# Couples of half products in the prologue of an attention and MLP block, and maxima that end three steps ahead of a group's first score instead of four

## The chip, the cores and the metric

The kernel runs on one core of a Trainium2 chip. The metric is the time of one execution on the device in microseconds, as the median of several runs; less is better. Before the change it is 1688.64 us, the median of three runs (1687.62 to 1691.29).

## What is computed

One transformer block over 2048 tokens of width 512, in float32, with 32 heads of width 16 and a hidden width of 1792. The condition vector gives six rows that shift, scale and gate.

```python
    def _A_ref(x, wqkv, wo):
...
        scale = Dh ** -0.5
        scores = jnp.einsum("bhqd,bhkd->bhqk", q, k) * scale
        p = _softmax(scores, axis=-1)
        o = jnp.einsum("bhqk,bhkd->bhqd", p, v)
...
    sa, ca, ga, sb, cb, gb = (mod[:, 0], mod[:, 1], mod[:, 2], mod[:, 3], mod[:, 4], mod[:, 5])
    h = _layernorm(x, axis=-1) * (1 + ca) + sa
    x = x + ga * _A_ref(h, A_wqkv, A_wo)
    h = _layernorm(x, axis=-1) * (1 + cb) + sb
    x = x + gb * _B_ref(h, B_w1, B_b1, B_w2)
```

`_B_ref` is Dense, Mish (`h * tanh(softplus(h))`), Dense.

## The kernel before

**Numbers.** Products that need more precision than TensorE's fast float32 gives are made from a high and a low part of each factor: three products (high by high, high by low, low by high) in one PSUM bank. `hi_copy` and `lo_sub` (L87 to L96) make the parts.

**Groups and steps.** Queries come in 4 blocks of 512 rows, heads in 8 groups of 4, which makes 32 groups of work. The main loop, `step(t)`, has 16 steps for a group, T = 512 in all. A step makes four score products (L618, a 128-key block by 512 queries, for two pairs of heads), their exponentials on ACT (L621), and the products with the values of two steps earlier (L636). The softmax needs the greatest score of each query. It is found beforehand from separate products (L569, followed by a reduce on DVE, L571); `neg_max` (L587) joins the parts, `max_rows` (L596) transposes them, and its `put` (L603) sends the rows by four DMAs on SP's queue into two spare rows of the query operand `qa`, so that a score product subtracts them itself. Maxima run PRO = 16 + LEAD = 20 steps ahead of the scores, with LEAD = 4. So the main loop starts with a prologue of 20 steps, t = -20 to -1, of maxima alone (`max_pair`, L575: two 64-row products into two adjacent banks, and one reduce, L585, over both), and ends with 20 steps of scores without maxima.

**Halves.** Score and maximum products use 64 of TensorE's 128 rows. The products of two heads lie in the two halves of the array and run beside each other. Dense products, those of the projections and the MLP, use all 128 rows. In the prologue they are issued whole by `whole_units` (L1291), up to 7.2 products of 512 columns (CREDIT) in each step, after the step's maxima. From t = 0 on each dense product is cut into two halves by `mm_half` (L129); each runs beside a score or a maximum in the other half of the array, the first half in an even step, the second in the next odd one. Two halves of one product add into the same bank, so the first of the second halves is given a dependency on an instruction of ACT that came after the first halves.

**How a step is filled.** `next_part` (L1272) gives every couple of steps (even, odd) `f` dense slots, six where there is dense work and none where there is none. A step has four maxima and four scores. `maxima` (L1310) deals the maxima out: 4 - o to the one half of the array (`mo`) and o to the other (`alone`), where o is `max(0, (8 - f) // 2)`: one with six dense slots, four with none. With PRO even, the two steps that share a set of maxima are also the two that share f.

**What sets the order.** There is no scheduler: every engine's queue is in the order in which the code is written. `at(h, f)` defers a function to half step h (`run_hooks`). Units of dense work stand in one queue in the order of `plan` (L1426): value, query and key projections of the later column slices, then weights and MLP. `planned` (L1431) asks for the split of a weight slice (`slice_split`, L233) into high and low part, which ACT casts and POOL subtracts, and for the next slice's load. `clear`, `store_at` and `load_at` (L188 to L199) move stores and loads away from the half steps around `put`.

**Buffers.** PSUM has eight banks: a ring of six for scores and maxima (`ring`, L151), `ms` and `acc`. A dense unit's `fin` empties its bank: for a query or key unit ACT copies it to `qf` (L258) and POOL makes `qh` and `ql` (L259, L260), each with two buffers, which DMAs then store; a value unit is copied once (L287).

Of the kernel before, what the change touches and what calls it, by code (L numbers as in the profile page):

```python
# [8 lines left out]
F32 = mybir.dt.float32  # L9
# [9 lines left out]
def adaln_block(ctx: ExitStack, tc: tile.TileContext, x, wqkv, wo, w1, b1, w2, c, w_mod, out):  # L19
# [18 lines left out]
    LEAD = 4  # L38
# [4 lines left out]
    CREDIT = 7.2  # L43
    LATE_SPLIT = {3: -8, 4: 4}
    LATE_LOAD = {3: -15, 4: -4, 5: 9}
# [101 lines left out]
    ring_at = [0]  # L147

    kept = []

    def ring(w=1):  # L151
        if w == 2 and ring_at[0] % 2:
            ring_at[0] += 1
        if kept and ring_at[0] % NRING == NRING - 1:
            ring_at[0] += 1
        b = ring_at[0] % NRING
        ring_at[0] += w
        return ring_t[:, b, :] if w == 1 else ring_t[:, b:b + 2, :]

    def bank(tag="ms"):  # L160
        return ring() if tag == "ring" else ps.tile([P, TB], F32, tag=tag, name="bk", bufs=1)

    def free_banks():
# [3 lines left out]
        for i in nc.cur_bb.bb.instructions:  # L167
# [12 lines left out]
            if banks:  # L180
                for j, b, others, theirs in seen[-32:]:
                    if j.engine != i.engine and not banks & b and not names & theirs and not made & others:
                        tc.declare_no_dep(i, j, reason="other banks")
                seen.append((i, banks, names, made))
# [3 lines left out]
    def clear(h):  # L188

        return h if h < 60 or h % 32 < 25 else h - h % 32 + 34  # L190

    def store_at(h):

        h = clear(h)
        return h if h < 60 or h % 32 < 22 else h - h % 32 + 27

    def load_at(h):

        return h if h < 60 or 4 <= h % 32 < 20 else h - h % 32 + 28 if 20 <= h % 32 <= 28 else h + -(h - 4) % 32  # L199
# [23 lines left out]
    slices = {}  # L223
    put_away = set()
# [17 lines left out]
    def qk_unit(kind, ct, tb, tag):  # L242
# [7 lines left out]
        def fin(h=None):  # L250
            qh = qp.tile([P, TB], F32R, tag="qh", name="qh", bufs=2)
            ql = qp.tile([P, TB], F32R, tag="ql", name="ql", bufs=2)
            if h is None:
                hi_copy("a", qh, acc)
                lo_sub("v", ql, acc, qh)
            else:
                qf = pw.tile([P, TB], F32, tag="raw", name="qf", bufs=1)
                nc.scalar.copy(qf, acc)  # L258
                hi_copy("p", qh, qf)  # L259
                lo_sub("p", ql, qf, qh)  # L260
# [314 lines left out]
    def max_pair(n, jq, kb):  # L575
# [9 lines left out]
        nc.vector.tensor_reduce(out=mxs[n][:, :, jq, kb:kb + 1], in_=pm, op=ALU.max, axis=AX.X)  # L585

# [722 lines left out]

    def maxima(n, u, s, others):  # L1310

        j, qs = divmod(u, 4)
        return ([max_tile(n, j, s, qs, kb) for kb in range(4 - others)],
                [max_tile(n, j, 1 - s, qs, kb) for kb in range(4 - others, 4)])

    def step(t):
# [4 lines left out]
        if t < 0:  # L1321

            for i in range(2):
                if tm < 16:
                    kb, jq = divmod(2 * tm + i, 8)
                else:
                    jq, kb = tm % 16 // 2, 2 * second + i
                max_pair(tm // 16, jq, kb)
            if second and tm % 16 == 15:
                neg_max(tm // 16)  # L1330
            run_hooks(2 * t + 1)
            for f in ats.pop(t, []):
                f()
            whole_units(2 * t + 1, CREDIT)
# [7 lines left out]
        if not second:  # L1342
            first_of["part"] = []
            if t == T - PRO:
# [12 lines left out]
        if tm < T:  # L1357
            o = max(0, (8 - f) // 2)
            mo, alone = maxima(tm // 16, tm % 16 // 2, s, o)

            mine = [x for p in zip(mo, own) for x in p] + own[len(mo):]
        else:
            o = max(0, (4 - f) // 2)
# [62 lines left out]
    plan = [(-PRO, 2, 0, range(4, 16)), (-PRO, 0, 1, (0,)), (-PRO, 1, 1, range(NB)), (-PRO, 1, 2, range(NB)),  # L1426
# [4 lines left out]
    def planned(i, a, tag):  # L1431
# [3 lines left out]
        def fin(h):  # L1435
            if a == args[-1]:
                if i + 2 < len(plan):
                    d = 4 if h > 0 else 1
                    split_at[i + 2] = LATE_SPLIT.get(i + 2, h + d)
                    at(split_at[i + 2], lambda: slice_split(*plan[i + 2][1:3], hi_eng="p" if h > 0 else "a"))  # L1440
# [60 lines left out]
    for i in range(EARLY):  # L1501
        at(3 * i - 37, lambda i=i: early_prep(i, 3 * i - 37))
# [25 lines left out]
    at(-3, lambda: load_v(0))  # L1528
# [9 lines left out]
    for pp, h in ((2, -22), (3, -2)):  # L1538
# [4 lines left out]

    for t in range(-PRO, T + 2):
# [35 lines left out]
```

## Time and profile before

| What | us |
|---|---|
| median of three runs | 1688.64 |
| the profiled execution's own time | 1688.32 |
| its span, from first to last instruction | 1686.5 |
| first maxima of the prologue | 47.45 |
| first scores | 98.95 |
| first step without maxima | 1530.80 |

The span is shorter than the execution's time by what lies before the first instruction and after the last. In the rows of the profile, PE is TensorE's matmuls, PEld its weight loads, DVE VectorE, ACT ScalarE, POOL GpSimd and SP the engine that issues the DMAs. A row of the timeline gives start, length, engine, line, operation, tiles and count, and in brackets how long the engine had been idle and what ended that. A matmul's length is from its start to its last result; since they are pipelined, the distance of two starts is the better measure of what one costs. A row of busy time by stretch gives each engine's busy time with its number of instructions, then the granted clock of TensorE, the DMA engines' busy share and GB/s.

### The profile page before, as it was taken

To read this page: it belongs to the slowest core of one execution; us is meant where nothing else is said; L and a number is where in the kernel's file an instruction comes from. 1 tells how busy PE (TensorE), PEld (TensorE's weight loads), DVE (VectorE), ACT (ScalarE), POOL (GpSimd) and SP (SyncE) were. 2 spreads that over 40 slices of the span, in tenths; PEclk is the share of its full clock that TensorE was granted. 3 is DMA by queue.
4 is the path that set the end of the run, shared out by engine and by line. 5 is a ranking of instruction groups with operands and counts; after the bars stand their busy time and mean duration, and the time that the engine had idled before them with its cause. 6 is when DMAs were issued, how large, how long until landed. Compare 5 with 4: busy or idle time off the path is not lost.

```text
span 1686.5 us, 33920 instructions
## 1 busy us (share of the span) xinstructions
PE 1670.4 (99%) x12491; PEld 924.4 (55%) x12491; DVE 1432.9 (85%) x2372; ACT 1357.4 (80%) x2612; POOL 812.5 (48%) x839
## 2 busy tenths in 40 slices
PE   8999999999999999999999999999999999999998
PEld 6755655555445455555555455555555455555687
DVE  6998888888999988888889888888889888883377
ACT  7257777777778988888878998888878988889674
POOL 5555224655313664556323565556323664555442
PEclk9999999999999999999999999999999999999999
DMA  8877656777755334434355434534344433534261
GB/s 261 264 251 188 157 145 197 205 228 218 225 136 161 97 93 104 120 81 130 82 137 161 106 77 98 139 80 122 100 133 120 130 93 81 149 97 135 76 227 63
DMA packets 114983, 239.00 MB, mean 142 GB/s; under 512 B 24500, under 2 KB 50120, under 8 KB 108864
## 3 DMA queue, kind: packets, MB, share of 16 engines
q1 hardware_dynamic: 114808, 236.82, 49.7%
q8 instruction: 99, 1.62, 0.4%
q14 instruction: 68, 0.56, 0.1%
q10 hardware_dynamic: 8, 0.00, 0.0%
HBM read 180.48 MB, written 51.45 MB: 138 GB/s over the span
## 4 chain that ended last, share of the span: by engine, by line
PE 92%; DVE 3%; ACT 2%; DMA 1%; issue 1%; POOL 0%; SPq 0%; ACTq 0%; DVEq 0%; POOLq 0%
PE bk L636 29%; PE ring L618 22%; PE ring L569 19%; PE bk L134 11%; PE bk L127 3%; PE ring L127 2%; PE ring L1249 2%; DVE mx L571 2%; ACT pr L621 1%; PE ring L583 1%; DMA qa<-mt 0%; PE ring L952 0%; PE ring L598 0%; DMA xt<-in_A_x 0%; PE ring L134 0%
## 5 line engine op out<-in xcount | busy, mean ns | idle before, releaser
L571 DVE TENSOR_REDUCE mx<-ring 128x1 f32<-128x512 f32 x1968 | 1221.9, 681 | 150.9 <-PE ring L569 136.2
L621 ACT ACTIVATE pr<-ring 128x512 f32<-128x512 f32 x2048 | 1078.7, 603 | 207.8 <-PE bk L134 116.3
L569 PE MATMUL ring<-ka,qa 64*128 64x512 f32 x1968 | 818.3, 429 | 1.3 <-ACT pr L621 1.0
L618 PE MATMUL ring<-qa,ka 64*128 64x512 f32 x2048 | 759.0, 402 | 3.2 <-ACT pr L621 2.0
L636 PE MATMUL bk<-pr,vg 128*32 128x512 f32 x4096 | 545.1, 604 | 0.0
L569 PEld LDWEIGHTS ring<-ka,qa 64*128 64x128 f32 x1968 | 350.6, 184 | 326.4 <-DVE mx L571 251.4
L618 PEld LDWEIGHTS ring<-qa,ka 64*128 64x128 f32 x2048 | 373.6, 184 | 192.2 <-DVE mx L571 113.3
L134 PE MATMUL bk<-h,w 64*128 64x512 f32 (+1 forms) x1080 | 277.8, 390 | 0.0
L134 PE MATMUL bk<-w,a_h 64*128 64x512 f32 x632 | 210.8, 413 | 0.0
L134 PEld LDWEIGHTS bk<-h,w 64*128 64x128 f32 x1080 | 178.5, 184 | 9.2 <-ACT pr L621 1.5
L636 PEld LDWEIGHTS bk<-pr,vg 128*32 128x32 f32 x4096 | 81.2, 108 | 135.8 <-issue 126.5
L134 PE MATMUL bk<-w,a_l 64*128 64x512 f32 x316 | 124.0, 392 | 0.0
L134 PEld LDWEIGHTS bk<-w,a_h 64*128 64x128 f32 x632 | 106.7, 184 | 3.4 <-ACT hb L830 0.8
L1008 POOL TENSOR_TENSOR y<-yd,y 128x512 f32<-128x512 f32 x44 | 56.8, 1292 | 88.9 <-ACT yd L1007 79.5
L842 POOL TENSOR_SCALAR qq<-ee 128x512 f32<-128x512 f32 x25 | 15.5, 620 | 169.3 <-ACT ee L836 169.3
L858 POOL TENSOR_TENSOR qq<-qq,rr 128x512 f32<-128x512 f32 x42 | 54.1, 1289 | 85.8 <-ACT rr L852 85.8
L844 POOL TENSOR_TENSOR hb<-hb,ee 128x512 f32<-128x512 f32 x42 | 54.1, 1288 | 79.6 <-DVE ee L840 77.6
L134 PE MATMUL bk<-w,o_hl 64*128 64x512 f32 x288 | 79.3, 405 | 0.0
L96 POOL TENSOR_TENSOR a_l<-hb,a_h 128x512 fp32r<-128x512 f32 x53 | 73.1, 1379 | 4.4
L134 PEld LDWEIGHTS bk<-w,a_l 64*128 64x128 f32 x316 | 58.3, 184 | 2.8
L93 POOL TENSOR_SCALAR qh<-qf 128x512 fp32r<-128x512 f32 x27 | 16.7, 620 | 88.3 <-ACT qf L258 68.1
L134 PE MATMUL bk<-h_h,wl 64*128 64x512 f32 x168 | 57.3, 421 | 0.2 <-ACT pr L621 0.2
(222 smaller groups left out, 1901.3 us busy)
## 6 DMA issues: line engine op xcount, KB each, us to landing
ka<-kscr SPq DMA_DIRECT2D x124, 384.0 KB
w<-w2scr SPq DMA_DIRECT2D x56, 512.0 KB
w<-w1scr SPq DMA_DIRECT2D x46, 512.0 KB
vg<-vscr SPq DMA_DIRECT2D x32, 552.0 KB
qa<-qscr SPq DMA_DIRECT2D x124, 100.0 KB
kscr<-qh SPq DMA_DIRECT2D x16, 512.0 KB
qscr<-qh SPq DMA_DIRECT2D x32, 256.0 KB
w2scr<-hl SPq DMA_DIRECT2D x14, 512.0 KB
```

The costliest lines, as they stand in the source:

```text
L96: (nc.gpsimd if eng == "p" else nc.vector).tensor_sub(lo, src, hi.bitcast(F32))
L127: nc.tensor.matmul(acc, l, r, start=start, stop=stop)
L134: i = nc.tensor.matmul(acc, l[64 * g:64 * g + 64], r[64 * g:64 * g + 64], start=start and not then, stop=bool(stop and then))
L569: nc.tensor.matmul(pm, qt[64 * s:64 * s + 64, qs * P:(qs + 1) * P], kt[64 * s:64 * s + 64, kb * TB:(kb + 1) * TB], start=True, stop=True)
L571: nc.vector.tensor_reduce(out=mxs[n][:, s, 4 * j + qs, kb:kb + 1], in_=pm, op=ALU.max, axis=AX.X)
L618: nc.tensor.matmul(p_, kt[64 * s:64 * s + 64, kc * P:(kc + 1) * P], qt[64 * s:64 * s + 64, :], start=True, stop=True)
L621: e = nc.scalar.activation(pr, p_, AF.Exp, scale=SCALE)
L636: nc.tensor.matmul(accs[n][32 * h:32 * h + 32, :], vgs[n][:, o:o + 32], pts.pop((t, h)), start=(kc == 0), stop=(kc == 15))
L844: (nc.vector if tail else nc.gpsimd).tensor_mul(hb, hb, ee)
L858: nc.gpsimd.tensor_mul(qq, qq, rr)
L1008: nc.gpsimd.tensor_add(y[i], yd, y[i])
L1249: nc.tensor.matmul(po[i // 2][:, i % 2, :], l[:, s], w[:, r, :], start=(f == 0 and j == 0), stop=(f == FT - 1 and j == 2))
```

## The change

Three things go together.

**Couples.** In the prologue dense work is issued by `lanes`. It takes units until it has 12 slots (one query or key unit, or two value units in one bank), twice, and calls these two takes a couple. `turn(c, 0)` issues one half of each product of the first take beside the other half of each product of the second; `turn(c, 1)` the halves that are left, later. Two couples alternate over four banks: the last two of the ring (which is shortened to four in the prologue), `ms` and `acc`. Six couples make up the prologue, four slots after each pair of maxima. So that the second halves have something to wait for, the first pair of maxima after a first turn is followed by a small copy on ACT (`seen`).

**Lead.** LEAD is 3, PRO is 19. The prologue and the end lose a step each, the steps with both maxima and scores gain one. `put` comes two half steps later against the scores, and the limits in `clear`, `store_at` and `load_at` move by two. Because PRO is odd, the two steps that share a set of maxima now lie in different couples of steps; o is kept from the first of them, and where f differs the step has uneven halves.

**Order and tiles.** The query unit of the second column slice comes before the value units, the split of a slice is issued at once in the prologue, and units that finish just before t = 0 get tiles of their own (`late`) for their parts.

```diff
-    LEAD = 4
+    LEAD = 3
     PRO = 16 + LEAD
...
     def qk_unit(kind, ct, tb, tag):
...
         def fin(h=None):
-            qh = qp.tile([P, TB], F32R, tag="qh", name="qh", bufs=2)
-            ql = qp.tile([P, TB], F32R, tag="ql", name="ql", bufs=2)
+            late = h is not None and -4 <= h < 3
...
+            if late:
+                qh, ql = spares.pop(), spares.pop()
+            else:
+                qh = qp.tile([P, TB], F32R, tag="qh", name="qh", bufs=2)
+                ql = qp.tile([P, TB], F32R, tag="ql", name="ql", bufs=2)
...
         nc.vector.tensor_reduce(out=mxs[n][:, :, jq, kb:kb + 1], in_=pm, op=ALU.max, axis=AX.X)
+        if waiting:
+            seen = ap.tile([P, 2], F32, tag="seen", name="seen", bufs=2)
+            e = nc.scalar.copy(seen, pm[:, :, 0])
+            for c in waiting:
+                c["after"] = e
+            waiting.clear()
...
+    COUPLES = 6
+    now, waiting = [0], []
+    beds = [ring_t[:, NRING - 2, :], ring_t[:, NRING - 1, :], "ms", "acc"]
...
+        def turn(c, p):
+            (a, fa), (b, fb) = c["two"]
+            for j, both in enumerate(zip(a, b)):
+                for k in range(max(len(x) for x in both)):
+                    for x, g in zip(both, (p, 1 - p)):
+                        if k < len(x):
+                            mm_half(x[k], g, c["after"] if p and not j and not k else None, p)
+                yield len(a) - j - 1
+            if not p:
+                waiting.append(c)
+                return
+            for fin in fa + fb:
+                at(now[0] + 1, lambda fin=fin, h=now[0] + 1: fin(h))
+
+        for _ in range(COUPLES // 2):
+            c1 = yield from couple()
+            yield from turn(c1, 0)
+            c2 = yield from couple()
+            yield from turn(c2, 0)
+            yield from turn(c1, 1)
+            yield from turn(c2, 1)
...
+    def dense_slots(h, most):
+
+        now[0] = h
+        for _ in range(most):
+            if not next(lane, 0):
+                return
...
     def maxima(n, u, s, others):
 
         j, qs = divmod(u, 4)
+        if (n, u) == (1, PRO % 16 // 2):
+            return ([max_tile(n, j, v, qs, kb) for kb in (2, 3)] for v in (s, 1 - s))
...
+                dense_slots(2 * t + 1, 4)
             for f in ats.pop(t, []):
                 f()
-            whole_units(2 * t + 1, CREDIT)
...
-            o = max(0, (8 - f) // 2)
+            o = mst["others"] = max(0, (8 - f) // 2) if tm % 2 == 0 or not t else mst["others"]
             mo, alone = maxima(tm // 16, tm % 16 // 2, s, o)
 
             mine = [x for p in zip(mo, own) for x in p] + own[len(mo):]
+            m = len(mine)
+            if f > m:
+                mine = [mine[(i * m) // f] if (i + 1) * m // f > i * m // f else None for i in range(f)]
...
-    plan = [(-PRO, 2, 0, range(4, 16)), (-PRO, 0, 1, (0,)), (-PRO, 1, 1, range(NB)), (-PRO, 1, 2, range(NB)),
+    plan = [(-PRO, 0, 1, (0,)), (-PRO, 2, 0, range(4, 16)), (-PRO, 1, 1, range(NB)), (-PRO, 1, 2, range(NB)),
...
-                    at(split_at[i + 2], lambda: slice_split(*plan[i + 2][1:3], hi_eng="p" if h > 0 else "a"))
+                    split = lambda: slice_split(*plan[i + 2][1:3], hi_eng="p" if h > 0 else "a")
+                    split() if h < -4 else at(split_at[i + 2], split)
...
+    ring_of[0] = NRING - 2
```

Where the instructions stand, at three places. First TensorE's queue at the start of the prologue, before the change (`ka`, `qa` are keys and queries, so those rows are maxima; `bk` is `ms` or `acc`; 128x256 is a value unit's product):

```order
L583 MATMUL ring<-ka_98,qa_100 128x512 x4
L127 MATMUL bk<-wh,h_h 128x256 x4
L127 MATMUL bk<-wl,h_h 128x256 x4
L127 MATMUL bk<-wh,h_l 128x256 x4
L127 MATMUL bk<-wh,h_h 128x256 x2
L583 MATMUL ring<-ka_98,qa_100 128x512 x4
```

Four maxima (two pairs) and then whole products of value units. The same place after the change, where a row is a half product or several:

```order
L595 MATMUL ring<-ka_98,qa_100 128x512 x2
L133 MATMUL ring<-h_h,wh 128x512
L133 MATMUL ring<-wh,h_h 128x256 x2
L133 MATMUL ring<-h_h,wh 128x512
L133 MATMUL ring<-wh,h_h 128x256 x2
L133 MATMUL ring<-h_h,wh 128x512
L133 MATMUL ring<-wl,h_h 128x256 x2
L133 MATMUL ring<-h_h,wh 128x512
L133 MATMUL ring<-wl,h_h 128x256 x2
L595 MATMUL ring<-ka_98,qa_100 128x512 x2
```

One pair of maxima, then four slots, each a half of the query unit's product beside two halves of a value unit's; the query unit has come to the front.

Second, ACT's queue in the first part of the prologue, before (`wh<-wr` is the cast of a weight slice, `vq<-bk` and `qf<-bk` empty the banks of value units and of query and key units):

```order
L89 CAST qh<-ring 128x512
L89 CAST wh<-wr 128x512
L287 COPY vq<-bk 128x4x4x16 x12
L89 CAST wh<-wr 128x512
L258 COPY qf<-bk 128x512 x3
```

The cast of the key slice comes after all twelve copies of value units. After the change:

```order
L88 CAST qh<-ring 128x512
L88 CAST wh<-wr 128x512
L600 COPY seen<-ring 128x2 x2
L88 CAST wh<-wr 128x512
L270 COPY qf<-ring 128x512
L299 COPY vq<-ring 128x4x4x16 x2
L299 COPY vq<-bk 128x4x4x16 x4
L600 COPY seen<-ring 128x2 x2
```

The same cast now stands ahead of the copies that empty the first couple's banks.

Third, TensorE's queue in the main loop, in the step in which the first unit of the output projection starts after a stretch without dense work, before (t = 128; `w,o_hl` are halves of that unit, `qa,ka` scores, `ka,qa` maxima); it starts behind two pairs of a score and a maximum, which are left out:

```order
L134 MATMUL bk<-w_5827,o_hl 128x512
L618 MATMUL ring<-qa_101,ka_99 128x512
L134 MATMUL bk<-w_5827,o_hl 128x512
L569 MATMUL ring<-ka_701,qa_103 128x512
L134 MATMUL bk<-w_5827,o_hl 128x512
L618 MATMUL ring<-qa_102,ka_700 128x512
L134 MATMUL bk<-w_5858,o_hl 128x512
L569 MATMUL ring<-ka_701,qa_103 128x512
L134 MATMUL bk<-w_5858,o_hl 128x512 x2
L618 MATMUL ring<-qa_101,ka_99 128x512
L636 MATMUL bk<-pr,vg 32x512 x4
```

Maxima and scores take turns beside the dense halves. After the change the stretch ends two steps earlier, and the whole step (t = 126) reads:

```order
L133 MATMUL bk<-w_5980,o_hl 128x512
L636 MATMUL ring<-qa_104,ka_702 128x512
L133 MATMUL bk<-w_5980,o_hl 128x512
L636 MATMUL ring<-qa_100,ka_98 128x512
L133 MATMUL bk<-w_5980,o_hl 128x512
L133 MATMUL bk<-w_6009,o_hl 128x512
L636 MATMUL ring<-qa_104,ka_702 128x512
L133 MATMUL bk<-w_6009,o_hl 128x512 x2
L636 MATMUL ring<-qa_100,ka_98 128x512
L581 MATMUL ring<-ka_701,qa_103 128x512 x4
L654 MATMUL bk<-pr,vg 32x512 x4
```

Only scores run beside the dense halves, and all four maxima stand in a row at the step's end, in the half of the array that held the dense work.

70 lines of the change are left out of this document (52 added, 18 removed).

## The prediction

> **What bounds the kernel now.** The page comes first: its span and busy shares.
>
> ```profile
> span 1686.5 us, 33920 instructions
> PE 1670.4 (99%) x12491; PEld 924.4 (55%) x12491; DVE 1432.9 (85%) x2372; ACT 1357.4 (80%) x2612; POOL 812.5 (48%) x839
> ```
>
> TensorE has no idle time worth the name, so time is won only where its work is issued more densely. The sum below is made against the profiled execution's own 1688.32 us, 0.32 below the median of 1688.64. The busy time by stage cuts the span at the first maximum of the prologue, the first score, and the last maximum.
>
> ```profile
> 47.45:98.95 51.50, 51.38 (x298) 36.62 (x298) 47.55 (x44) 9.82 (x22) 29.87 (x28) 1.00 0.84 274
> 98.95:1530.80 1431.85, 1425.82 (x11051) 749.20 (x11051) 1267.94 (x2140) 1213.37 (x2371) 690.67 (x688) 1.00 0.50 136
> 1530.80:1583.30 52.50, 52.50 (x401) 26.59 (x401) 7.90 (x16) 46.22 (x91) 30.73 (x29) 1.00 0.21 72
> ```
>
> After each length stand PE, PEld, DVE, ACT and POOL. The prologue's 20 steps take 51.50 us (2.58 each), the 492 middle steps 2.91 each, the 20 steps without maxima 2.63 each. DVE is busy 47.55 of the prologue's 51.50, so it is the second bound there. One prologue step in order of time, matmuls first, then the weight loads behind the two changes of shape:
>
> ```profile
> 75.78 0.73 PE L583 MATMUL ring<-ka,qa 64*128 64x512 f32 x4
> 76.44 0.50 PE L127 MATMUL bk<-h_h,wl 128*128 128x512 f32 x1
> 76.78 1.08 PE L127 MATMUL bk<-h_l,wh 128*128 128x512 f32 x4
> 77.70 0.63 PE L127 MATMUL bk<-h_h,wh 128*128 128x512 f32 x2
> 78.26 0.73 PE L583 MATMUL ring<-ka,qa 64*128 64x512 f32 x4
> ```
> ```profile
> 76.44 0.19 PEld L127 LDWEIGHTS bk<-h_h,wl 128*128 128x128 f32 x1 [0.36 <-issue]
> 78.26 0.30 PEld L583 LDWEIGHTS ring<-ka,qa 64*128 64x128 f32 x4 [0.36 <-issue]
> ```
>
> Four 128-row products start in 0.92 us (76.78 to 77.70), 0.23 each. The step has seven of them and two pairs of 64-row maxima, nine slots of 0.23 or 2.07 us, but it lasts 2.48: 0.41 goes into the two changes of shape, about 0.2 each, at which the weight loader sits idle for 0.36 with nothing to wait for.
>
> **The prologue, part by part.** Dense products in 64-row halves, two units side by side, take the shape of the maxima, so the changes of shape go. What such a slot costs the middle steps show, where a half of a dense product runs beside a score or a maximum:
>
> ```profile
> 430.20 0.39 PE L618 MATMUL ring<-qa,ka 64*128 64x512 f32 x1
> 430.20 0.39 PE L134 MATMUL bk<-h_h,wl 64*128 64x512 f32 x1
> 430.43 0.39 PE L569 MATMUL ring<-ka,qa 64*128 64x512 f32 x1
> 430.66 0.39 PE L618 MATMUL ring<-qa,ka 64*128 64x512 f32 x1
> ```
>
> Two halves start together, and a slot again takes 0.23. The new prologue has 19 steps of two calls; a call is one pair of maxima and four dense slots. Six couples make 144 slots, 36 calls with dense work and two without (one comes up empty where the second key slice is not split yet, one at the end). 36 calls of 5 x 0.23 = 1.15 make 41.4 us. The two bare ones cost between 0.23 (PE) and 1.15 (the reduces, below); I take 0.5 each, 1.0 together. DVE must keep up:
>
> ```profile
> 48.83 9.27 DVE L585 TENSOR_REDUCE mx<-ring 128x2 f32<-128x1024 f32 x8
> ```
> ```profile
> L585 DVE TENSOR_REDUCE mx<-ring x40: 1212/1216/1227, 48.8 to 98.2; 128x2 f32<-128x1024 f32 x40
> ```
>
> Queued reduces start (9.27 - 1.22) / 7 = 1.15 us apart though each lasts 1.22, so DVE's floor of 38 x 1.15 = 43.7 us lies beside PE's 41.4 and its waits. Three waits come in. First, the start:
>
> ```profile
> 48.09 0.62 ACT L89 CAST wh<-wr 128x512 fp32r<-128x512 f32 x1
> 48.12 0.74 PE L127 MATMUL bk<-wh,h_h 128*128 128x256 f32 x4
> 48.79 1.29 POOL L96 TENSOR_TENSOR wl<-wr,wh 128x512 fp32r<-128x512 f32 x1 [2.10 <-ACT wh L89]
> ```
>
> Today the first dense unit is a value unit whose weights lie ready; the query unit, whose weights this cast and subtraction make, comes much later. Now it is first: PE is free at 47.45 + 0.23 = 47.68, the cast ends at 48.71, the subtraction at 50.08. That is 1.1 us at the first slot and 0.2 at the fifth, 1.3 together; between 0.6 and 1.5. Second, the banks of couple 1:
>
> ```profile
> 59.24 0.43 SPq L230 DMA_DIRECT2D wr<-in_A_wqkv  x1
> 59.78 1.54 SPq L1488 DMA_DIRECT2D ep<-in_B_w  x3
> ```
> ```profile
> 63.54 0.62 POOL L93 TENSOR_SCALAR ep<-ep 128x512 fp32r<-128x512 f32 x1 [8.22 <-DMA ep<-in_B_w]
> 49.86 0.37 ACT L287 COPY vq<-bk 128x256 f32<-128x256 f32 x1 [1.15 <-PE bk L127]
> 77.95 0.59 ACT L258 COPY qf<-bk 128x512 f32<-128x512 f32 x1 [3.60 <-PE bk L127]
> ```
>
> When the query unit is done, ACT is given the cast of the key slice ahead of that unit's copy, and the slice is the load of 59.24. Queued behind that cast are the copies that empty couple 1's two banks, and couple 3 wants those banks at call 12, 47.45 + 1.3 + 12 x 1.15 = 62.55. The load's landing is not shown; the one issued right behind it is awaited until 63.54, so it lies between 60.6 and 63.5. With 62.3, the cast (0.62), the query copy (0.59) and a value copy (0.37) end at 63.9, a wait of 1.35 for PE; with the ends, 0 to 2.5. Third, the way out: the transposes of the maxima still change shape, and the main loop's step 0 has eight slots instead of seven and enters on banks that the last reduces free.
>
> ```profile
> 89.26 0.28 PE L598 MATMUL ring<-ident,mm 128*32 128x128 f32 x1
> ```
>
> 0.28 and two changes of 0.2 make 0.7; step 0's slot (0.23) and some 0.5 of reduces make another 0.7 (0.2 to 1.9, a reduce and a half). Sum: 41.4 + 1.0 + 1.3 + 1.35 + 0.7 + 0.7 = 46.45 us for 51.50, **5.05 less**, and one step of maxima is left to the main loop.
>
> **The main loop.** That step costs 2.91 and replaces a last step of 2.63: **+0.28**. With an odd lead the two steps that share one set of maxima lie in different couples of steps. Where the dense work stops or starts between them (five times each), the first step without dense work has 7 slots instead of 4, and the first with dense work 10 instead of 7: 3 x 0.23 = 0.69 more each. Here is the first such stretch; the rows are the first weight load of a step.
>
> ```profile
> 432.70 0.18 PEld L569 LDWEIGHTS ring<-ka,qa 64*128 64x128 f32 x1 [0.84 <-DVE mx L571]
> 435.59 0.18 PEld L618 LDWEIGHTS ring<-qa,ka 64*128 64x128 f32 x1 [0.84 <-DVE mx L571]
> 437.55 0.18 PEld L618 LDWEIGHTS ring<-qa,ka 64*128 64x128 f32 x1 [0.84 <-ACT pr L621]
> 440.28 0.18 PEld L618 LDWEIGHTS ring<-qa,ka 64*128 64x128 f32 x1 [0.84 <-ACT pr L621]
> ...
> 468.03 0.18 PEld L618 LDWEIGHTS ring<-qa,ka 64*128 64x128 f32 x1 [0.84 <-ACT pr L621]
> 471.36 0.18 PEld L569 LDWEIGHTS ring<-ka,qa 64*128 64x128 f32 x1 [0.84 <-DVE mx L571]
> ```
>
> A dense step takes 2.89, the first bare one 1.96, the next 2.73: by then PE waits for ACT and DVE. With 7 slots the first takes 1.96 + 0.69 = 2.65, but leaves no backlog, so the 1.96 comes one step later: the two make 4.61 against 4.69, nothing. The first dense step takes 3.33 today, 0.44 of it waiting; with 10 slots 2.89 + 0.69 = 3.58, 0.25 more. I take 0.35 a stretch, **+1.75** for five; the bounds are 0.25 (1.25) and twice 0.69 (6.9).
>
> **Maxima three steps ahead.** Their rows reach the score's operand by four DMAs; here are the DMAs of one group, the load that follows, and the group's first score; then the slowest landing, from the chain, and all that scores waited for it.
>
> ```profile
> 1396.96 2.77 SPq L607 DMA_DIRECT2D qa<-mt  x4
> 1399.83 0.33 SPq L781 DMA_DIRECT2D w<-w1scr  x1
> ```
> ```profile
> 1404.86 0.19 PEld L618 LDWEIGHTS ring<-qa,ka 64*128 64x128 f32 x1
> ```
> ```profile
> 369.97 7.91 DMA qa<-mt
> ```
> ```profile
>   DMA qa<-mt: 0.9, 1
> ```
>
> 7.90 us lie between issue and score; a step of 2.84 less leaves 5.06. Where landing took 7.91, the queue held stores issued earlier; they keep their places while the DMAs move two half steps behind them, so it should be done at the same time as now. I price this at 0 (0 to 17, a rival below). Each wait of SP, and each load or store that now stands ahead of these DMAs, is covered by the same 5.06 us.
>
> Sum: 1688.32 - 5.05 + 0.28 + 1.75 = 1685.3, and with the 0.32 to the median **1685.6**. Own range of this case, from the waits' bounds: 1683.8 to 1687.3. A measurement of this kernel can tell about 0.2%, 3.4 us, from no change: below 1685.3 it is faster.
>
> **Rivals.** (1) No wait but the start: couple 1's banks are free in time, reduces never lag, and stretches cost their lower bound. 5.05 + 1.35 + 0.7 + 0.5 (the bare calls) = 7.6 less, plus 0.28 and 1.25: 1682.6. For it: DVE's floor fits in PE's time. Against: the load of 59.24.
> (2) The reduces set the prologue's pace: they do not queue, and each takes its full 1.216. 38 of them are 46.2, after a first start 1.38 behind PE's, with couple 1's wait of 1.35 and step 0's 0.7: 49.6, only 1.9 less, or 1688.8. Against it stands the spacing of 1.15. [...]
> (3) The mismatched steps cost their full price: 6.9 instead of 1.75, 1690.8. For it: engines are in order, and four maxima now follow the dense halves at a step's end. Against: today's steps there already wait.
> (4) Slower: the DMAs of the maxima land too late. In six groups the load that stands behind them today (the 1399.83 row) is issued just ahead. It decides from a landing of 5.06 us on; with 7.91 a group's scores wait 2.85, six times 17.1: 1702.7. For it: that landing was seen once. Against: of 32 groups one waits now, 0.9 us, and 5.06 is long for 4 KB.
>
> **Chances.** Forecast 0.45, rival 1 0.20, rivals 2 and 3 0.12 each, rival 4 0.11. Faster: 0.19 of the forecast, rival 1 and a little of 2, 0.40. Slower: rival 4 and a quarter of rival 3, 0.14. The same: 0.46. The range of 1681.3 to 1691.5 takes in rivals 1 to 3 and leaves out rival 4 and some tails.
>
> **What would show it.** Right: the first score at 93 to 95 us after the span's start; no idle rows of 0.36 between maxima and dense products; a stop of PE of about 1.3 us near 62.5, ended by ACT; steps of 3.5 to 3.7 where dense work starts; no more than a few us of scores waiting for these DMAs. Wrong: a first score after 97, reduces 1.22 apart throughout, or waits for these DMAs in many groups.

## The result and the profile after

The changed kernel takes 1710.28 us (median of 4 runs, 1708.76 to 1711.48) beside 1689.7 for the kernel before, run with it: a ratio of 1.0127, 95% interval 1.0114 to 1.0140. It is slower by about 21 us, where the prediction said 1685.6 with a range up to 1691.5. The profiled execution took 1708.76 us. Its first lines, and the same cuts by stage as before (first maxima, first score, first step without maxima, last score step; columns as in the prediction: length, then PE, PEld, DVE, ACT, POOL, the granted clock, the share of the DMA engines and GB/s):

```profile
span 1707.0 us, 34378 instructions
PE 1677.7 (98%) x12707; PEld 941.2 (55%) x12707; DVE 1432.9 (84%) x2373; ACT 1358.7 (80%) x2619; POOL 812.3 (48%) x839
```
```profile
47.85:105.85 58.00, 48.68 (x511) 43.18 (x511) 45.70 (x42) 8.85 (x27) 30.45 (x30) 0.94 0.81 253
105.85:1553.48 1447.63, 1438.76 (x11070) 761.13 (x11070) 1271.12 (x2144) 1216.37 (x2374) 692.74 (x690) 1.00 0.49 134
1553.48:1604.00 50.52, 50.43 (x383) 25.61 (x383) 6.81 (x14) 44.77 (x87) 27.65 (x26) 1.00 0.22 74
```

The prologue has one step less and is 6.50 us longer (58.00 for 51.50). The loop with maxima has one step more, 493, and is 15.78 longer (1447.63 for 1431.85); the last part has 19 steps for 20 and is 1.98 shorter. With 0.40 at the start and 0.2 less at the end this is the whole difference of the spans, 20.5. TensorE is idle for 9.3 of the prologue's 58.00 us. Here are its stops of over 0.4 us, each with its length and what ended it in brackets; the first lies just ahead of the prologue:

```profile
47.85 0.59 PE L595 MATMUL ring<-ka,qa 64*128 64x512 f32 x2 [1.45 <-DMA ka<-kscr]
65.67 0.38 PE L133 MATMUL ring<-wh,h_h 64*128 64x256 f32 x1 [1.67 <-ACT qf L270]
88.19 2.12 PE L133 MATMUL bk<-h_h,wh 64*128 64x512 f32 x8 [3.58 <-ACT vq L299]
91.22 1.60 PE L133 MATMUL bk<-h_h,wl 64*128 64x512 f32 x6 [0.48 <-POOL wl L95]
98.44 0.50 PE L595 MATMUL ring<-ka,qa 64*128 64x512 f32 x2 [0.56 <-DVE mx L597]
105.85 0.49 PE L636 MATMUL ring<-qa,ka 64*128 64x512 f32 x1 [2.46 <-DMA qa<-mt]
```

These stops cost more than their length. The granted clock (the third column from the right, 1.00 is full) in the stretch behind the first stop, in the undisturbed one after it, behind the stop of 3.58, and, from a second answer, behind the one of 2.46 and behind a wait of 3.02 us in the main loop:

```profile
47.80:51.80 4.00, 3.94 (x27) 3.95 (x29) 2.41 (x3) 0.00 (x0) 4.00 (x3) 0.57 0.85 311
51.80:63.80 12.00, 12.00 (x170) 11.88 (x166) 11.47 (x11) 0.32 (x2) 2.38 (x2) 1.00 0.51 167
88.20:92.60 4.40, 3.92 (x17) 2.48 (x19) 1.23 (x1) 0.49 (x2) 4.23 (x5) 0.62 1.06 394
```
```profile
105.90:109.40 3.50, 3.50 (x16) 2.75 (x18) 1.62 (x3) 2.17 (x4) 0.93 (x1) 0.56 1.05 377
387.10:391.10 4.00, 4.00 (x18) 2.49 (x22) 2.63 (x4) 2.37 (x4) 2.02 (x3) 0.50 0.82 214
```

At 0.57 for 4.00 us, 4.00 x 0.43 = 1.7 us of work are lost, at 0.62 for 4.40 again 1.7, at 0.56 for 3.50 1.5. The means between 0.5 and 1 come from where the rows are cut: the clock is at exactly 0.50 from 48.27 to 51.68, from 89.23 to 92.64, from 106.30 to 109.71 (3.41 us each) and from 386.19 to 393.02 (6.83), and at 1.00 between these. "PE busy" counts this as work, so only the clock's column shows it. Away from the stops the couples do what was reckoned. Two rows eight calls apart, and the reduces behind them:

```profile
67.15 0.51 PE L595 MATMUL ring<-ka,qa 64*128 64x512 f32 x2
...
76.55 0.44 PE L595 MATMUL ring<-ka,qa 64*128 64x512 f32 x2
```
```profile
67.70 18.66 DVE L597 TENSOR_REDUCE mx<-ring 128x2 f32<-128x1024 f32 x16 [2.44 <-PE ring L595]
```

A call takes (76.55 - 67.15) / 8 = 1.175 us, and the reduces follow (18.66 - 1.23) / 15 = 1.16 us apart. At that pace 36 calls with dense work are 42.3 of the 58.00; the stops inside the prologue are 1.67 + 3.58 + 0.48 + 0.56 + 2.46 = 8.75, the slow clock 3.4, and 3.5 are left for two bare calls, the transposes and step 0.

In the main loop the first stretch without dense work looks like this (first weight load of each step; the prediction shows the same steps of before):

```profile
444.47 0.18 PEld L581 LDWEIGHTS ring<-ka,qa 64*128 64x128 f32 x1 [0.84 <-DVE mx L583]
447.37 0.19 PEld L581 LDWEIGHTS ring<-ka,qa 64*128 64x128 f32 x2 [0.84 <-DVE mx L583]
449.25 0.20 PEld L636 LDWEIGHTS ring<-qa,ka 64*128 64x128 f32 x2 [0.84 <-ACT pr L639]
452.83 0.18 PEld L636 LDWEIGHTS ring<-qa,ka 64*128 64x128 f32 x1 [0.84 <-ACT pr L639]
...
474.73 0.18 PEld L636 LDWEIGHTS ring<-qa,ka 64*128 64x128 f32 x1 [0.84 <-ACT pr L639]
478.89 0.18 PEld L581 LDWEIGHTS ring<-ka,qa 64*128 64x128 f32 x1 [0.84 <-ACT pr L639]
```

The two steps at its start take 1.88 + 3.58 = 5.46 where they took 4.69, the first dense step 4.16 where it took 3.33: 0.77 and 0.83 more, 1.6 a stretch and 8.0 if all five cost the same. The loop's 15.78 are then 2.91 for its own additional step, 8.0 for the stretches, and 4.9 of which nearly all lies at one group. Set step against step with the kernel before, the loop agrees with that sum: 4.7 us are lost in the two steps around group 6's first score, and 8.0 from there to the end, though in uneven portions (1.7 at the stretch shown). The waits of scores for the maxima's DMAs, and the chain's two longest landings of them:

```profile
PE ring L636 <- DMA qa<-mt: 5.5, 2, 3.0
```
```profile
98.70 7.11 DMA qa<-mt
379.88 7.08 DMA qa<-mt
```

One of the two waits is group 0's (2.46, in the prologue's list), the other group 6's (3.02, for 0.9 before), with the clock at 0.50 behind it as shown: about 2.1 us of the 4.7 are the longer wait, and 2.6 the clock.

### The profile page after: what moved, and what is told of

It reads as the page before. It is cut to its first block, busy times and chain, and to the rows that moved or that the text cites. A ratio compares the mean times of both kernels' runs of the same rounds, so it can differ in the third digit from the quotient of the medians.

```text
span 1707.0 us, 34378 instructions
## 1 busy us (share of the span) xinstructions
PE 1677.7 (98%) x12707; PEld 941.2 (55%) x12707; DVE 1432.9 (84%) x2373; ACT 1358.7 (80%) x2619; POOL 812.3 (48%) x839
## 4 chain that ended last, share of the span: by engine, by line
PE 89%; DVE 4%; DMA 3%; ACT 2%; issue 1%; SPq 0%; POOL 0%; ACTq 0%; DVEq 0%; POOLq 0%
PE bk L654 29%; PE ring L636 21%; PE ring L581 19%; PE bk L133 12%; DVE mx L583 2%; PE ring L1267 2%; PE ring L126 2%; PE bk L126 1%; ACT pr L639 1%; DMA qa<-mt 1%; PE ring L133 1%; DMA ep<-in_B_w 1%; DMA kscr<-ql 0%; PE ring L970 0%; DVE mx L597 0%
## 5 line engine op out<-in xcount | busy, mean ns | idle before, releaser
L133 PEld LDWEIGHTS bk<-w,a_h 64*128 64x128 f32 x632 | 106.8, 184 | 3.9 <-ACT hb L848 0.4
L133 PE MATMUL bk<-h_h,wl 64*128 64x512 f32 x192 | 63.9, 432 | 0.6 <-POOL wl L95 0.5
L133 PE MATMUL bk<-h_h,wh 64*128 64x512 f32 x192 | 55.4, 420 | 3.8 <-ACT vq L299 3.6
```

What stands on the lines that cost most here:

```text
L133: i = nc.tensor.matmul(acc, l[64 * g:64 * g + 64], r[64 * g:64 * g + 64], start=start and not then, stop=bool(stop and then))
```

## The experiments

All ratios are to runs of the kernel before on the same chip, where its median was between 1687.84 and 1689.7 us; so times of two rows are comparable to about 2 us only. "First score" and "prologue" are read from each profile.

| kernel | us, median | ratio, 95% interval | first score | prologue |
|---|---|---|---|---|
| before | 1689.7 | | 98.95 | 51.50 |
| changed | 1710.28 | 1.0127 (1.0114 to 1.0140) | 105.85 | 58.00 |
| three ahead, whole products | 1700.50 | 1.0074 (1.0060 to 1.0088) | 99.09 | 52.7 |
| couples, four ahead | 1696.61 | 1.0050 (1.0037 to 1.0063) | 105.00 | 57.3 |
| bounds of stores put back | 1706.62 | 1.0106 (1.0091 to 1.0122) | 107.7 | 59.8 |
| idle products, half rows | 1710.94 | 1.0137 (1.0121 to 1.0154) | 106.35 | 58.5 |
| idle products, all rows | 1707.25 | 1.0106 (1.0092 to 1.0119) | 107.32 | 59.3 |
| other bank pair first | 1707.78 | 1.0102 (1.0089 to 1.0116) | 104.4 | 58.4 |
| slices: later cast, earlier load | 1709.37 | 1.0122 (1.0108 to 1.0135) | 109.4 | 61.0 |
| no early preparations | 1723.25 | 1.0197 (1.0182 to 1.0212) | 99.25 | 50.5 |
| four ahead, two preparations | 1717.57 | 1.0164 (1.0150 to 1.0178) | 99.5 | 51.9 |
| the same, slices moved | 1719.60 | 1.0179 (1.0162 to 1.0197) | 102.0 | 53.6 |
| four ahead, early stream | 1696.99 | 1.0046 (1.0033 to 1.0060) | 106.8 | 60.4 |
| the same, splits later | 1687.72 | 0.9996 (0.9987 to 1.0005) | 95.76 | 48.2 |

**The two halves apart.** Couples with a lead of four:

```diff
-    LEAD = 3
+    LEAD = 4
...
-        if (n, u) == (1, PRO % 16 // 2):
+        if PRO % 2 and (n, u) == (1, PRO % 16 // 2):
...
-            o = max(0, (4 - f) // 2) if t > T - PRO else 0
+            o = max(0, (4 - f) // 2)
```

> The changed kernel with maxima four steps ahead again (lead 4; the bounds on stores and loads, the end of the maxima and the early preparations put back with it), couples kept. Theory A (each mismatched stretch costs its full price, about 1.6 us twice over five stretches, 7.9 in all, and the short lead makes group 6 wait 3.0 us plus about 1.7 at half clock): 7.9 + 4 go, one prologue step of 2.3 comes and 0.3 goes, 1710.3 falls to about 1700. Theory B (the loss of the main loop comes from something that the couples left behind in it, the lead is innocent): no more than 2 us go, 1707 to 1712. The waits inside the prologue at the key slices stay in both.

And the lead alone, in the kernel before:

```diff
-    LEAD = 4
+    LEAD = 3
...
-    CREDIT = 7.2
+    CREDIT = 7.6
...
-            o = max(0, (8 - f) // 2)
+            o = mst["others"] = max(0, (8 - f) // 2) if tm % 2 == 0 or not t else mst["others"]
```

> The kernel before with maxima three steps ahead and all that this needs (bounds, the shared odd steps), but with whole products in the prologue as before, 7.6 slots a step instead of 7.2. Theory A (the main loop's loss belongs to the lead alone): the mismatched stretches (7.9), group 6's wait with its slow clock (4.7) and the tail (1.3) come in full, one prologue step without its dense part goes (about 1.2): 1700 to 1703. Theory B (the loss needs the couples): within 3 us of the kernel before, 1687 to 1692.

Theory A's times held in both, the first with 3 us less than it said. The start of the first score and of the steps without maxima, first with four ahead and couples, then with three ahead and whole products (there the score is line 618):

```profile
105.00 0.76 PE L636 MATMUL ring<-qa,ka 64*128 64x512 f32 x1 [3.51 <-DMA qa<-mt]
1540.25 0.18 PEld L133 LDWEIGHTS bk<-h,w 64*128 64x128 f32 x1 [0.84 <-ACT pr L639]
```
```profile
99.09 0.50 PE L618 MATMUL ring<-qa,ka 64*128 64x512 f32 x1 [1.66 <-DMA qa<-mt]
1545.15 0.18 PEld L134 LDWEIGHTS bk<-h,w 64*128 64x128 f32 x1 [0.84 <-ACT pr L621]
```

With four ahead the loop takes 1435.25 for 492 steps, 3.4 more than before. Of these 2.6 are lost in its first two steps, in which the clock is 0.50 behind that last stop (in both rows from 105.00 to 112.00), and 0.6 at group 6. With three ahead it takes 1446.06 for 493, as in the changed kernel (1447.63), though there are no couples. So the loop's loss belongs to the lead, and nearly all of the prologue's (57.3 and 58.00; 52.7 with whole products) to the couples. The halves add up: 0.50% and 0.74% are 1.24%, for 1.27% together. Theory A's price for group 6 did not come in full, though: with whole products the wait there is 2.18 at full clock, and 1.2 us are lost where the changed kernel loses 4.7. Another 1.6 are lost in one step near 120 us.

**The rows of the maxima.** The change also moves three bounds that keep stores and loads clear of the maxima's DMAs. They were put back:

```diff
-        return h if h < 60 or h % 32 < 27 else h - h % 32 + 34
+        return h if h < 60 or h % 32 < 25 else h - h % 32 + 34
-        return h if h < 60 or h % 32 < 24 else h - h % 32 + 29
+        return h if h < 60 or h % 32 < 22 else h - h % 32 + 27
-        return h if h < 60 or 4 <= h % 32 < 20 else h - h % 32 + 30 if 20 <= h % 32 <= 30 else h + -(h - 4) % 32
+        return h if h < 60 or 4 <= h % 32 < 20 else h - h % 32 + 28 if 20 <= h % 32 <= 28 else h + -(h - 4) % 32
```

> The changed kernel with the three bounds that keep stores and loads clear of the maxima's DMAs put back by two half steps, to where they stood for a lead of four; nothing else. Theory A (the traffic moved with the maxima, so the landing still took 7.3 us and met a shorter slack; with the bounds back it ends earlier): group 6's wait of 3.0 us shrinks to 1 or less and its slow clock with it, about 1706. Theory B (the traffic's place does not matter, the queue is full whatever the order): group 6 waits as before, 1710.

Theory A for the most part: 3.7 us less (0.21% by the ratios). Group 6 waits 1.47 for 3.02 and its clock stays at 1.00. But group 7, which did not wait, now waits 1.94, also at full clock (and with the DMA engines 0.18 busy from 433 to 435, in the wait): with the shorter slack the wait is in another group. The edit leaves the prologue as it was, and yet this profile's prologue is 1.8 us longer, with a stop of 5.14 at the third slice for 3.58: so much one stop varies from execution to execution.

**The clock.** Idle products fill the two waits for these rows. In the first of these runs they used 64 rows, and in group 6 they stand behind the first score instead of ahead of it:

```diff
+            for _ in range({0: 10, 6: 12}.get(n, 0) if (j, s, kc) == (0, 1, 0) else 0):
+                nc.tensor.matmul(p_, kt[64:128, :P], kt[64:128, :TB], start=True, stop=True)
```

> The changed kernel with 10 idle products ahead of group 0's first score and 12 ahead of group 6's, into the bank that the score then overwrites; they fill the two waits for the DMAs of the maxima and compute nothing that is used. Theory A (PE's clock falls because PE stops): the granted clock stays near 1.0 behind both waits and the 1.6 and 1.9 us lost there are won back, about 1707. Theory B (the slow stretch behind a wait has another cause, DMA traffic or power): clock and time stay, 1710, or the products cost up to 2 us more.

Inconclusive. In group 0 the products covered 2.56 us of the wait and left 0.69, and the clock still fell, to 0.52; that half rows are too little work to hold it, or that the rest of the wait was enough, this run doesn't tell. The second run:

```diff
+            if n in (0, 6) and all(a // 16 != n for a, _ in pts):
+                for _ in range(13):
+                    nc.tensor.matmul(p_, h_h[:, 0, :P], h_h[:, 0, :TB], start=True, stop=True)
```

> The changed kernel with 13 products of all 128 rows ahead of the very first score of groups 0 and 6 in TensorE's order, into the bank that the score overwrites (the earlier run of this kind used half rows, and in group 6 stood behind the first score). Theory A (the clock falls because PE stops): the granted clock stays above 0.9 in the 4 us behind both waits, and 3 us come back, about 1707. Theory B (it falls for another reason): it is 0.5 to 0.6 there as before, 1710.

Theory A. Behind both waits (104.15 to 107.32 and 384.87 to 388.04 are the idle products) the clock is full:

```profile
107.30:111.30 4.00, 3.47 (x26) 2.56 (x26) 2.98 (x5) 2.83 (x6) 0.40 (x1) 1.00 1.06 404
```
```profile
388.50:392.50 4.00, 4.00 (x36) 2.29 (x32) 3.56 (x6) 2.85 (x6) 3.20 (x3) 1.00 1.01 199
```

The DMA engines are no less full than in the changed kernel (1.06 and 1.01 for 1.05 and 0.82), so at these two places it is TensorE's standing still that lowers its clock, not the traffic. 3.0 us come back with products that compute nothing.

**The first maxima's bank.** While the couples hold two of the six score banks, the ring turns over four, and the counter, at 22 by then, points to bank 22 mod 4 = 2, where the last key product lies (20 mod 6 = 2); in the ring of six it pointed to banks 4 and 5.

```diff
     ring_of[0] = NRING - 2
+    ring_at[0] += 2
```

> The changed kernel with the ring of score banks moved on by one pair before the prologue, so that the first maxima don't enter the bank that still holds the last key product (the four-bank ring of the change puts them there, the six-bank ring of before did not). The wait of 1.45 us for DVE's subtraction ahead of the first maxima goes in any case, and the half clock behind it where there was one. Theory A (the prologue is a chain of its own work): 1.5 to 3.1 us less, 1707 to 1709. Theory B (the later stops are set by the DMAs and POOL, which run by their own time): the stops at 84 us and at the first score grow by as much, first score still 105 to 106 and time 1710.

In line with theory A, 2.5 us less, but the intervals of the two ratios still touch (1.0116 and 1.0114). The maxima start at 46.08 without a wait, and PE waits 0.80 for the query slice's cast instead. In the changed kernel's page this wait was put down to a DMA that came last; seven of the eight other profiles with the same wait name DVE's subtraction from that bank.

**The slices.** The third key slice comes late. The casts go behind the copies of the banks, and the slice's load ahead:

```diff
-    LATE_LOAD = {4: -4, 5: 9}
+    LATE_LOAD = {3: -26, 4: -4, 5: 9}
-                    split() if h < -4 else at(split_at[i + 2], split)
+                    at(split_at[i + 2], split)
```

> The changed kernel with the cast of a key slice queued one half step later, behind the copies of the couple's banks, and the third slice's load moved ahead, behind the first four early preparations. Theory A (the two stops of PE in the middle of the prologue are waits for ACT's cast, which waits for the slice): the stops of 1.67 and 3.58 us go and with the second the half clock behind it (about 1.6) and the wait for the subtraction (0.5), 7 us in the prologue; what of it is seen at the end depends on the rows of the maxima, whose landing the full DMA queues set: 1703 to 1707. Theory B (the DMAs or the reduces set the prologue's end, the stops only show them): the first score stays at 105 to 106 us and the time at 1710.

Theory A's wins did not come, and theory B's first score (109.4) is not right either: ACT's two waits went, and POOL's took their place. PE, then POOL:

```profile
71.65 0.79 PE L133 MATMUL bk<-h_h,wl 64*128 64x512 f32 x1 [3.91 <-POOL wl L95]
96.02 2.07 PE L133 MATMUL bk<-h_h,wl 64*128 64x512 f32 x7 [7.95 <-POOL wl L95]
```
```profile
90.85 0.62 POOL L92 TENSOR_SCALAR ep<-ep 128x512 fp32r<-128x512 f32 x1 [6.60 <-DMA ep<-in_B_w]
91.55 1.26 POOL L95 TENSOR_TENSOR ep<-ep 128x512 fp32r<-128x512 f32 x1
92.78 0.62 POOL L92 TENSOR_SCALAR qh<-qf 128x512 fp32r<-128x512 f32 x1
93.48 1.26 POOL L95 TENSOR_TENSOR ql<-qf,qh 128x512 fp32r<-128x512 f32 x1
94.70 1.26 POOL L95 TENSOR_TENSOR wl<-wr,wh 128x512 fp32r<-128x512 f32 x1
```

The third slice's cast on ACT had been done at 84.0 (83.39 and 0.64 us long), but on POOL the slice's subtraction (`wl`) stands behind the split of an early preparation (`ep`), which waits 6.60 us for its load.

**The early preparations.** So these were taken out of the prologue, in the changed kernel, all six; the main loop does them with the others.

```diff
-    EARLY = 6
+    EARLY = 0
```

> The changed kernel without the six early preparations of first-layer weights in the prologue (they are done in the main loop with the others): each is a load of 256 KB, a split on POOL and two stores. Theory A (these preparations make the prologue's stops: their traffic delays the third key slice, their splits stand ahead of the slices' subtractions on POOL, their stores delay the rows of the maxima): the waits at 84.6 us (3.58), for the subtraction (0.5) and for the maxima's rows (2.46) go with the half clock behind them (1.6 and 1.6), 9.8 us, first score near 96; 1710.3 falls to 1699 to 1703. Theory B (the slices and the rows are late by themselves): the first score stays above 102 and the time above 1707. Group 6's wait and the mismatched stretches stay in both.

Theory A for the prologue, though its first score is at 99.25 and not near 96: the waits at 84.6 us and for the subtraction are gone, and the one for the rows of the maxima is 0.69. That leaves these stops of PE:

```profile
48.78 0.57 PE L595 MATMUL ring<-ka,qa 64*128 64x512 f32 x2 [1.44 <-DVE ql L95]
65.34 0.38 PE L133 MATMUL ring<-wh,h_h 64*128 64x256 f32 x1 [1.95 <-ACT qf L270]
93.67 0.50 PE L595 MATMUL ring<-ka,qa 64*128 64x512 f32 x2 [0.60 <-DVE mx L597]
```
```profile
99.25 0.50 PE L636 MATMUL ring<-qa,ka 64*128 64x512 f32 x1 [0.69 <-DMA qa<-mt]
```

50.5 us for 58.00: 7.5 us of the changed prologue came from the traffic and the POOL work of six preparations. But the kernel is 13 us slower. Its attention ends 12 us earlier than the changed kernel's (last products of probabilities and values at 1593.0 for 1604.9), and behind it stand 124.8 us for 102.1, among them one stop:

```profile
1612.11 1.22 PE L126 MATMUL bk<-w,a_h 128*128 128x512 f32 x2 [10.67 <-POOL a_h L92]
```

What isn't prepared early is missing at the other end: of the second layer's products that used to run beside the attention 30 more are left to do alone (488 matmuls in all behind it, for 454), and behind the stop two products together take 1.22 us and a single one 0.80, where those ahead of it took 0.62 and 0.40. With a lead of four, two preparations give the same picture (the end takes 124.4), and with two the moved slices only shift the stop (3.81 for `wl` at the second slice):

```diff
-    EARLY = 6
+    EARLY = 2
```

> The couples with a lead of four (1696.6) and two early preparations instead of six. Theory A: as above, the waits of 2.41 and 3.51 us in its prologue go with their slow clock (1.6 each), first score near 97 instead of 105.0 and the time 1687 to 1690. Theory B: no more than 2 us less, 1695.

> The run with two early preparations, and with it the slices' casts one half step later, behind the copies of the banks, and the third slice's load moved ahead behind the two early loads. Theory A: with POOL nearly free nothing takes the place of ACT's wait now; the stop at the second slice (1 to 1.7 us) goes too, and the prologue runs at its slot pace from the first maxima on, first score 94 to 96, 1684 to 1688. Theory B (each wait that goes hands its place to another, as with the early slice and six preparations): no less than the run beside it, 1687 to 1690 or more.

In both the sum was wrong by the end of the kernel, which neither theory had reckoned with.

**All six, but earlier.** The DMA engines are half idle early in the prologue (0.51 from 51.80 to 63.80), as SP, which issues nothing from 54.75 to 59.20, stands behind the loads of the last quarter of the keys, which wait for their stores. With a lead of four, the other bank pair, and the slices' casts and third load moved as in the run before, those loads went behind the preparations':

```diff
+                if tb + 1 < NB:
+                    load_k(pp, tb)
+                else:
+                    at(-34, lambda pp=pp: load_k(pp, NB - 1))
...
-        at(h + 7, split)
-        at(h + 10, put)
+        at(h + 5, split)
+        at(h + 7, put)
...
-        at(3 * i - 37, lambda i=i: early_prep(i, 3 * i - 37))
+        at(1 * i - 39, lambda i=i: early_prep(i, 1 * i - 39))
```

> The couples with a lead of four, the other bank pair for the first maxima, all six early preparations kept but begun earlier: the key columns that only the last quarter of the first maxima reads are loaded behind the first five weight loads instead of ahead of them, so that SP does not stand still for their stores from 54.7 to 59.2 us, the splits follow five half steps after their loads instead of seven, and the third slice's load and the casts stand as in the run with two preparations. Theory A (the prologue's stops are late loads and POOL's queue, not the couples): the stops at the second and third slice and at the first score shrink to under 1 us each, first score 94 to 98, and with the main loop of a lead of four and all preparations done the time is 1684 to 1689. Theory B (the DMAs are full and only change places): first score above 102, 1693 or more.

By the numbers theory B, by the profile one stop: 9.92 us at the second slice, whose subtraction now stood behind all six splits on POOL, and behind the parts of a query unit. The last run moves the splits (from 5 half steps behind their loads to 12), with them the stores, and the third slice's load by one half step:

```diff
-    LATE_LOAD = {3: -28, 4: -4, 5: 9}
+    LATE_LOAD = {3: -27, 4: -4, 5: 9}
...
-        at(h + 5, split)
-        at(h + 7, put)
+        at(h + 12, split)
+        at(h + 14, put)
```

> As the early stream, but POOL's splits of the early preparations stand twelve half steps behind their loads, so that the second slice's subtraction comes ahead of all of them in POOL's queue; there it stood behind five of them and stopped PE for 9.92 us. Theory A (that one place in POOL's order is all that is left): the stop goes with the slow clock behind it (1.7 and more), first score 94 to 97, time 1684 to 1688, faster than the kernel before or equal to it. Theory B (another queue takes the place, as three times already): first score above 100, 1691 or more.

Theory A: the prologue takes 48.2 us, 3.3 less than in the kernel before, with no stop at the second or third key slice; only the query slice's 0.81 at the start is left. Here are its first score and the two rows behind it, in which the clock falls once more, to 0.54 and 0.50, amid four waits of 0.60 to 0.64 us between 88.7 and 96.9:

```profile
95.76 0.47 PE L639 MATMUL ring<-qa,ka 64*128 64x512 f32 x1 [0.62 <-DMA qa<-mt]
```
```profile
96.00:100.00 4.00, 3.36 (x15) 2.14 (x13) 3.38 (x5) 1.90 (x4) 1.72 (x2) 0.54 1.07 393
100.00:104.00 4.00, 3.71 (x15) 2.46 (x14) 2.27 (x5) 2.09 (x4) 0.00 (x0) 0.50 0.98 289
```

These two give back 4.00 x 0.46 + 4.00 x 0.50 = 3.8 us in the profiled execution. At group 6 it loses another 2.7, with a wait of 2.30 and a clock of 0.56 in the 3.50 us behind it. This execution took 1692.14 us, the most of eleven; the median is equal to the kernel before (0.9996). No version that beats it came out of these runs.

## Why the prediction was wrong

**The prologue's pace was right.** 36 calls were put at 41.4 us and come to 42.3 at the measured pace; the changes of shape are gone. DVE and PE bound a call nearly alike (1.16 and 1.175), so rival 2's full 1.216 for each reduce did not come about: it is a tie.

**Couple 1's wait was right.** Put at 1.35 near 62.5, it is 1.67 at 64.00, ended by ACT's copy behind the cast.

**The waits counted were not all there were.** The sum had three. It followed the second slice's load, but not the third's, although the diff deletes that slice's own times (`LATE_SPLIT`, `LATE_LOAD`): 3.58 + 0.48. The wait put at 1.3 for the query slice at the start was not there; another was, 1.45 for the bank, in front of the first maxima, and it hid the first, which shows as 0.80 once the bank is free (other bank pair). And none of the work on POOL and on the queues that is not part of the couples, the six preparations, was set against the earlier times at which the couples need their slices; the run without them shows that this is most of the loss.

**A stop was priced at its length.** In the changed kernel the stops of 1.45, 2.46, 3.02 and 3.58 us lost another 1.7, 1.5, 2.6 and 1.7 us at a lower clock. The main loop of the kernel before has one stop of 0.94 and stays at full clock (1.00). But the same profile has the clock at 0.50 from 23.29 to 26.71, ahead of the prologue and behind a stop of 1.32 that ends at 21.44, and the prediction made nothing of it; the rivals' waits were too small by it as well.

**The maxima's rows.** "Priced at 0, since the stores keep their places" failed. Landing takes 7.1 us in two groups (7.91 in one before), and the slack is shorter; the stores did not keep their places, since the diff moves their bounds with the maxima. Rival 4 had the mechanism, but in the wrong six groups: it is groups 0 and 6, where stores and long loads stand ahead, and not those with a weight load. Group 0 waits with four ahead too (3.51 with couples), so only group 6's wait is the lead's.

**The mismatched steps.** "The 1.96 comes one step later, nothing" failed. The two steps cost 0.77 more, the first dense step 0.83 instead of the 0.25 that was reckoned for it. A bare step already runs at ACT's and DVE's pace (2.73 us before, of which four reduces of 0.68 take 2.72); a step of seven slots with nearly all of them in one half of the rows keeps both waiting (ACT stands 1.06 us for a score in it), and what these two lose, 1.6 us a stretch, is not won back in it. This was rival 3, at 6.9; it came to about 8.0, with the first dense step at 4.16 and not 3.5 to 3.7.

In sum, for 20.5 us: start 0.4, prologue 6.5 (put at -5.05), one step more and one less 0.28, stretches 8.0 (1.75), group 6 and small change 4.9 (0), the 19 last steps 0.65 more than their share, the end -0.2.

## What to carry to other kernels

When a stage is made denser, every queue that feeds it has to be as early as the new pace needs: list all that stands ahead of each input on each queue (POOL and SP above all), not only the step's own work. In the run with later casts and an earlier load the third slice's cast was done at 84.0, and its subtraction began at 94.70, behind a preparation for which POOL had waited 6.60 us. And expect that a wait taken away hands its place to the next, as the 1.67 and 3.58 us for ACT did to 3.91 and 7.95 for POOL there. Work that fills a prologue's idle queues may be paid for at the far end when it is taken out: without the six preparations the prologue was 7.5 us shorter and the part behind the attention 22.7 longer (124.8 for 102.1). And a diff's bounds and tables are part of the change: what they move shares the queues with what the change is about.

## What the runs showed of the hardware

In the traces of the kernel before and of the changed one the granted clock is either 1.00 or 0.50; rows that are cut wider show means such as 0.57. From the prologue to the last scores the changed kernel has four stretches at 0.50, three of 3.41 us and the one at group 6 of 6.83. Three begin behind the end of a stop of TensorE: 0.42 us behind the one of 1.45, 1.04 behind the one of 3.58 and 0.45 behind the one of 2.46. The fourth begins within the stop of 3.02 (at 386.19, with the score at 387.10). In the kernel before one begins 1.85 us behind the stop of 1.32 that ends at 21.44.

From the prologue to the last scores all these profiles together have 16 stops of 2.30 us or more, and with 15 of them the rows show a lower clock: 0.56 in the 3.50 us behind the shortest (2.30, four ahead with the splits later), 0.50 in the 3.46 behind the longest (9.92, four ahead with the early stream). The exception had 2.94, with 1.00 behind it (later cast, earlier load, group 6). Between 1.4 and 2.3 us it went either way. Behind the stop of 1.44 or 1.45 at the start the clock was 0.55 to 0.57 in four profiles and 1.00 in five; it was 0.61 behind one of 1.66 (three ahead, whole products) and 0.55 behind one of 1.97 (other bank pair), and 1.00 behind others of 1.67, 1.94 and 2.18. Behind stops of 0.94 and 1.04 it was 1.00; but four of 0.60 to 0.64 within 8.2 us went with the 0.54 and 0.50 shown above.
